# Thresholded attention and a gated feed-forward block on one core: the order of all tasks sought anew, with other durations for four kinds of task

## The chip, the core and the metric

The kernel runs on one core of a Trainium2 chip. A core has a matrix engine (PE, called TensorE), a vector engine (DVE), a scalar engine (ACT), a general engine (POOL, called GpSimd) and a sequencer for transfers (SP, called SyncE). Each takes its own instructions in the order in which they were written into its list, and waits on semaphores for the others. On-chip memory is SBUF (128 partitions); PE writes its results into PSUM. The metric is the device time of one execution in microseconds (us), the median over runs; less is better.

## What is computed

The reference first does attention on 8 batches of 8 heads, 576 positions and 64 values a head, keeping only scores within tau of the row's maximum, and then a feed-forward block on the 4608 rows that result.

```python
scores = scale * np.matmul(q, k.transpose(0, 1, 3, 2))
thresh = np.max(scores, axis=-1, keepdims=True) - tau
scores = np.where(scores >= thresh, scores, -1000000000.0)
scores = scores - np.max(scores, axis=-1, keepdims=True)
attn = np.exp(scores)
attn = attn / (np.sum(attn, axis=-1, keepdims=True) + 1e-09)
x = np.matmul(attn, v)            # (8, 8, 576, 64), then turned into (4608, 512)
h = x @ w_in                      # (512, 2048)
g = h * (1.0 / (1.0 + np.exp(-1.702 * h)))
return g @ w_out                  # (2048, 512)
```

All of it is in float32.

## The kernel before

**The work on a pair of heads.** Heads are taken in 32 pairs, n = 0 to 31, four to a batch. SP loads q, k and v (`load_qk`, L446 to L457, and `load_v`, L468). For the first four pairs PE turns q and k with a unit matrix (`turn_in`, L565 and L568) and ACT and DVE copy the result out of PSUM (`turned`, L580 and L578); for the later ones DVE turns them (`prep`, L556). PE forms the scores, transposed, in nine pieces (`scores`, L590). ACT copies each piece into SBUF (`keep`, L607), so that a pair has four full tiles of 1152 columns and one half tile of 576. DVE takes the maximum of each tile (`in_groups`, L613) and over the tiles (`over_tiles`, L622). The maximum over the partitions is an exchange between groups of 32: ACT copies four (or two) small pieces across (`cross_max`, L632) and DVE joins them (`over_halves`, L639). The result is spread over a tile on DVE (`spread_max`, L651), or, for pair 1 and pairs 3 to 6, sent through DRAM by transfers of POOL (L646, L647, L663, L672), which for some tiles are also added to the scores by an accumulating transfer (`add_row`, L678). DVE subtracts it (`sub`, L687), ACT does the mask (`mask`, L694) and the exponential (`exps`, L698). PE multiplies with v (`values`, L709). The row sums are products with a matrix of ones for the first four pairs (`sums_by_pe`, also L709, results in `den`); for later pairs DVE adds (`in_groups`, L613, `over_tiles`, L622), ACT exchanges (`cross_sums`, L764), DVE inverts (L769 to L773) and transfers send the row out and back spread (`sums_out`, L778, and `sums_in`, L785). DVE scales the values with it and places them as the input of the feed-forward block (`place_x`, L813).

**One block of PE for two pairs.** From pair 6 on, the values of an earlier pair and the scores of pair n are one block of PE: eight L709 and eight L590 in turn, nothing else between them. From pair 7 on the earlier pair is n - 1. Up to pair 16 such a block begins when all exponentials of the earlier pair are over.

**The weights.** w_in and w_out come in 16 pieces each (`load_w`, L510), and each piece is converted by two steps on ACT (`cv_power`, L520, and `cv_power2`, L524) and two on DVE (`cv_whole`, L538, and `cv_end`, L545).

**The feed-forward block.** It goes over the 4608 rows in blocks of 256. The first two blocks are plain products: L876 and L887 for the first matrix, with ACT (`tanh`, L843) and DVE (`gelu_0`, L893) behind them, L856 for the second, copied out by ACT (`half`, L863). All later ones take seven products of quarters in place of eight (L955, L1097, L1248 for the first matrix; L1397, L1357 for the second), with sums of quarters on DVE and ACT (L969, L974, L1013 to L1024, L1419). For this, sums of quarters of the weights are built once: ACT copies a quarter (`w_copy`, L922, for w_in; `t_minus`, L997, for w_out), and an accumulating transfer of POOL adds the other (`w_plus`, L926, and `t_plus`, L1001, 1 MB each). There are four of each, and each waits for the one before.

**Products of ones.** PE also does 88 small products of a matrix of ones with itself (`stay_warm`, L1463, 44 tasks of two), whose results are not used. They have the lowest rank of all.

**What sets the order.** The kernel builds a list of tasks, each with its engine, a duration in us, a rank, the tasks that it waits for and the buffers that it takes and gives back. `run_in_order` then plays this list through with the durations that the tasks carry: whenever an engine is free, the ready task of least rank runs next, and its instructions are written into the engines' lists at that moment. The order is thus fixed when the kernel is built; the chip doesn't change it. A task's rank is the number of its pair plus a bias by the name of its function: `EARLY` for pairs 0 to 3, `SECOND` for 4 to 7, `LATER` from 8 on, `CV` for weight pieces. `W_RANK` and `L_RANK` rank the loads of weights and of q, k and v. Products of the feed-forward block have the rank `LAST` (1000): PE does them when no attention task is ready.

```python
if rank != FIRST and rank < LAST and f not in (first_act, tau_terms, run_up, stay_warm):
    biases = EARLY if a[0] < NPAIR else SECOND if a[0] < 2 * NPAIR else LATER
    rank += CV[f.__name__] if f.__name__ in CV else biases.get(f.__name__, 0.0)
```

Of the kernel before, what the change touches and what calls it, by code (L numbers as in the profile page):

```python
# [32 lines left out]
def kernel(  # L33
# [96 lines left out]
    for x in ("raw0", "raw1", "qkT0", "qkT1", "mb"):  # L130
# [6 lines left out]
        "add_row": -16.97,  # L137
        "cross_max": -20.65,
        "exps": 41.44,
        "in_groups": -70.53,  # L140
        "keep": -47.19,
        "load_qk": 48.52,
        "load_v": 47.71,
        "mask": 87.96,
        "one_row": 0.3,
        "over_halves": 0.45,
        "over_tiles": -10.52,
        "place_x": 37.44,
        "row_in": 46.59,
        "row_out": 59.74,  # L150
        "scores_run": -87.56,
        "spread_max": 71.07,
        "spread_sums": 153.92,
        "sub": 40.08,
        "sums_by_pe": 1.52,
        "turn_in": 15.11,
        "turn_rows": 0.21,
        "turned": 66.22,
        "values": 60.02,
    }  # L160
    SECOND = {
        "add_row": -30.98,
        "cross_max": -5.57,
        "cross_sums": 40.19,
        "exps": 292.23,
        "in_groups": 939.1,
        "keep": -76.76,
        "load_qk": 18.7,
        "load_v": 63.05,
        "mask": 42.23,  # L170
        "over_halves": -41.03,
        "over_tiles": -26.57,
        "place_x": -8.57,
        "prep": 26.61,
        "row_in": 40.59,
        "row_out": 35.52,
        "scores_run": -43.88,
        "spread_max": -18.91,
        "sub": 135.33,
        "sums_in": 34.0,  # L180
        "sums_out": 41.84,
        "turn_rows": 96.96,
        "turn_sums": 176.66,
        "values": 15.56,
    }
    LATER = {
        "add2": -35.99,
        "add3": -111.96,
        "copy2": -83.6,
        "copy3": -8.15,  # L190
        "cross_max": 47.26,
        "cross_sums": 50.04,
        "exps": 44.03,
        "in_groups": 94.92,
        "keep": -19.43,
        "load_qk": 20.35,
        "load_v": -38.75,
        "mask": -10.73,
        "over_halves": 16.72,
        "over_tiles": 100.01,  # L200
        "place_x": 73.6,
        "prep": 141.22,
        "s_level1": -14.23,
        "s_level2": -24.56,
        "scores_run": 9.16,
        "silu2": -52.07,
        "spread_max": -56.97,
        "sub": 11.52,
# [2307 lines left out]
```

## Time and profile before

| | us |
|---|---|
| runs of the kernel before: median (lowest, highest of 3) | 1228.22 (1226.78, 1228.65) |
| the profiled execution, its own time | 1225.56 |
| span of the profile of that execution | 1223.8 |
| ACT busy, whole span | 800.8 |
| DVE busy, whole span | 1059.3 |
| mean traffic to and from the DMA engines | 112 GB/s |

A row in order of time gives the start in us from the beginning of the span, the duration, the engine, the line, the operation, what it writes and reads, the shape, and how many instructions were merged into it; in brackets stands how long the engine had been idle before it, and what ended that. "PEld" is the load of the fixed operand of a matmul, "q" behind an engine's name its sequencer. PE's instructions overlap each other, so one of them is longer than the pace at which they follow. One product in the kernel is two matmuls in the trace, as the operands are float32. A buffer is named without its number: `arena` stands for two large regions that hold most tiles.

### The profile page before, as it was taken

To read this page: it belongs to the slowest core of one execution; us is meant where nothing else is said; L and a number is where in the kernel's file an instruction comes from. 1 tells how busy PE (TensorE), PEld (TensorE's weight loads), DVE (VectorE), ACT (ScalarE), POOL (GpSimd) and SP (SyncE) were. 2 spreads that over 40 slices of the span, in tenths; PEclk is the share of its full clock that TensorE was granted. 3 is DMA by queue.
4 is the path that set the end of the run, shared out by engine and by line. 5 is a ranking of instruction groups with operands and counts; after the bars stand their busy time and mean duration, and the time that the engine had idled before them with its cause. 6 is when DMAs were issued, how large, how long until landed. Compare 5 with 4: busy or idle time off the path is not lost.

```text
span 1223.8 us, 26074 instructions
## 1 busy us (share of the span) xinstructions
PE 1211.3 (99%) x10592; PEld 980.2 (80%) x10592; DVE 1059.3 (87%) x1649; ACT 800.8 (65%) x1201; POOL 71.9 (6%) x115
## 2 busy tenths in 40 slices
PE   8999999999999999999999999999999999999999
PEld 6557764587888888887777877787887797999999
DVE  6898987778889998999879786788789889999797
ACT  6999998576676767665677376747875676440340
POOL 0111222110000000000000010001100000000000
PEclk9999999999999999999999999999999999999999
DMA  8848659873313233233432242224422341344443
GB/s 218 218 99 220 171 154 181 191 153 75 109 30 109 48 88 81 74 97 102 122 84 69 71 125 74 75 54 118 101 50 67 98 128 53 125 130 135 146 135 104
DMA packets 202232, 137.12 MB, mean 112 GB/s; under 512 B 146880, under 2 KB 164416, under 8 KB 201984
## 3 DMA queue, kind: packets, MB, share of 16 engines
q1 hardware_dynamic: 189712, 110.21, 33.7%
q0 software_dynamic: 11712, 24.95, 9.9%
q8 instruction: 83, 1.36, 0.5%
q10 hardware_dynamic: 688, 0.30, 0.1%
q14 instruction: 37, 0.30, 0.1%
HBM read 103.28 MB, written 23.75 MB: 104 GB/s over the span
## 4 chain that ended last, share of the span: by engine, by line
PE 80%; issue 1%; ACT 0%; DMA 0%; DVE 0%; POOL 0%; POOLq 0%; DVEq 0%; ACTq 0%
PE ops L1397 24%; PE pv L709 9%; PE ps L590 8%; PE hps L955 7%; PE hps L1097 7%; PE ps L955 5%; PE ps L1097 5%; PE ops L1357 4%; PE hps L1248 4%; PE ps L1248 3%; PE ps L1357 3%; DMA arena<-row_s 0%; ACT arena L694 0%; DVE arena L687 0%; ACT arena L698 0%
## 5 line engine op out<-in xcount | busy, mean ns | idle before, releaser
L613 DVE TRANSPOSE_TENSOR_REDUCE part<-arena 128x36 f32<-128x1152 f32 (+1 forms) x300 | 365.0, 1241 | 75.0 <-ACT arena L607 58.5
L607 ACT COPY arena<-ps 128x576 f32<-128x576 f32 x288 | 170.9, 642 | 112.0 <-PE ps L590 111.6
L694 ACT ACTIVATE arena<-arena 128x1152 f32<-128x1152 f32 (+1 forms) x160 | 165.9, 1062 | 55.8 <-DVE arena L687 55.5
L687 DVE TENSOR_TENSOR arena<-arena 128x1152 f32<-128x1152 f32 (+1 forms) x150 | 180.4, 1243 | 0.7
L698 ACT ACTIVATE arena<-arena,shift 128x1152 f32<-128x1152 f32 (+1 forms) x160 | 178.9, 1154 | 1.2
L590 PE MATMUL ps<-arena 64*64 64x288 f32 x2304 | 172.1, 410 | 5.4 <-ACT arena L607 2.6
L1397 PE MATMUL ops<-w_out,arena 128*128 128x256 f32 x768 | 173.1, 380 | 0.0
L1397 PEld LDWEIGHTS ops<-w_out,arena 128*128 128x128 f32 x768 | 144.7, 190 | 23.0 <-issue 3.9
L709 PE MATMUL pv<-arena 64*64 64x288 f32 x2176 | 158.1, 405 | 0.0
L590 PEld LDWEIGHTS ps<-arena 64*64 64x64 f32 x2304 | 83.3, 133 | 65.4 <-ACT arena L607 19.9
L709 PEld LDWEIGHTS pv<-arena 64*64 64x64 f32 x2176 | 80.4, 133 | 52.8 <-issue 7.5
L1397 PE MATMUL ops<-arena 128*128 128x256 f32 x528 | 118.5, 380 | 0.0
L1397 PEld LDWEIGHTS ops<-arena 128*128 128x128 f32 x528 | 100.1, 190 | 14.8 <-issue 1.3
L632 ACT ACTIVATE other<-red,minus_gap 32x18 f32<-32x18 f32 x118 | 36.2, 307 | 52.4 <-DVE red L622 51.1
L1262 ACT COPY arena<-hps 128x512 f32<-128x512 f32 x44 | 25.8, 585 | 59.3 <-PE hps L1248 58.8
L856 PE MATMUL ops<-w_out,arena 128*128 128x512 f32 x128 | 55.9, 594 | 0.0
L1074 POOL DMA_DIRECT2D arena<-wrow x36 | 19.4, 540 | 592.4 <-PE ops L1397 395.7
L887 PE MATMUL hps<-xT,w_in 128*128 128x256 f32 x232 | 50.8, 380 | 0.0
L887 PEld LDWEIGHTS hps<-xT,w_in 128*128 128x128 f32 x232 | 43.9, 190 | 6.8 <-issue 0.9
L856 PEld LDWEIGHTS ops<-w_out,arena 128*128 128x128 f32 x128 | 24.1, 190 | 30.1 <-issue 28.9
L955 PEld LDWEIGHTS hps<-xT,w_in 128*128 128x128 f32 x384 | 44.4, 192 | 1.1 <-issue 0.5
L955 PE MATMUL hps<-xT,w_in 128*128 128x128 f32 x384 | 45.1, 275 | 0.1
(228 smaller groups left out, 1909.2 us busy)
## 6 DMA issues: line engine op xcount, KB each, us to landing
arena<-in_v_dram SPq DMA_DIRECT2D x128, 144.0 KB
arena<-exu SPq DMA_DIRECT2D x42, 256.0 KB
arena<-ext SPq DMA_DIRECT2D x39, 256.0 KB
arena<-wrow POOLq DMA_DIRECT2D x36, 256.0 KB, 3.0
arena<-in_k_dram SPq DMA_DIRECT2D x112, 72.0 KB
arena<-in_q_dram SPq DMA_DIRECT2D x112, 72.0 KB
out_dram<-osb SPq DMA_DIRECT2D x28, 256.0 KB
arena<-row_s SPq DMA_DIRECT2D x48, 144.0 KB
```

The source lines that it names most:

```text
L590: nc.tensor.matmul(ps[ts(c, KT), h, 0:SH], lhsT=mats[n, 1][ts(h, D), ts(j, KT)], rhs=mats[n, 0][ts(h, D), ts(c, SH)], start=True, stop=True,)
L607: nc.scalar.copy(out=sT[n, t][:, u], in_=pss.pop((n, j))[:, :, 0:SH])
L613: nc.vector.tensor_reduce(out=stats[n, op][:, t * 2 * QB : min(2 * t + 2, NK) * QB], in_=sT[n, t].rearrange("p u h (g d) -> p (u h g) d", ...
L687: engine.tensor_tensor(out=s, in0=s, in1=mbs[n].unsqueeze(1).to_broadcast(list(s.shape)), op=ALU.add if n in BY_DMA else ALU.subtract,)
L694: nc.scalar.activation(out=s, in_=s, func=AF.Prelu, alpha=STEEP)
L698: nc.scalar.activation(out=s, in_=s, func=AF.Exp, scale=SCALE, bias=shift)
L709: nc.tensor.matmul(o[c][ts(h, D), 0:SH], lhsT=left(j, h)[ts(c, KT)], rhs=sT[n, t][ts(c, KT), u, h, :], start=(j == 0), stop=(j == NK - 1),)
L887: nc.tensor.matmul(hidden[j][:, ts(i, BLK)], lhsT=w_in[:, c, ts(j, P)], rhs=xTs[i][:, c, :], start=(c == 0), stop=(c == NDC - 1), skip_gro ...
L955: nc.tensor.matmul(o[:, ts(j, HT)], lhsT=left[:, c, ts(4 * y + j, P)], rhs=right[:, c, :], start=(x in (P1, P2, P5) and j + c == 0), stop= ...
L1097: nc.tensor.matmul(o[:, ts(j, BLK)], lhsT=left[:, c, ts(j, P)], rhs=right[:, c, :], start=(x in (P1, P2, P5) and j + c == 0), stop=(j + c ...
L1248: nc.tensor.matmul(o[:, ts(j, HT)], lhsT=left[:, ts(j, P)], rhs=right, start=(m in (P1, P2, P5) and j == 0), stop=(j == 3), skip_group_che ...
L1397: nc.tensor.matmul(banks[blk][k][:, ts(o, HM)], lhsT=left[:, j, :], rhs=right[:, j, :], start=(j == 0), stop=(j == HF - 1),)
```

## The change

The code of every task is the same. Changed are numbers in the tables of biases, the ranks of the loads, the durations of some tasks in the list, and one dependence: the small products of ones no longer wait each for the one before, only for the first one.

- All values of `EARLY`, `SECOND`, `LATER` and `CV`, of `W_RANK` and of `L_RANK` are new.
- `cross_max` (the exchange of maxima): 0.45 to 0.55 where two pieces are exchanged, 0.85 to 1.2 where four are.
- `cv_power` 0.68 to 0.75 and `cv_power2` 0.65 to 0.56.
- `turn_in` of pairs 1 to 3: 0.75 and 1.3 to 0.6 and 1.2.
- `stay_warm`: 0.25 to 0.26.

```diff
     LATER = {
-        "add2": -35.99,
-        "add3": -111.96,
...
+        "add2": -48.46,
+        "add3": -25.71,
...
-    W_RANK = (127.9, 169.1, 75.25, 398.03, -20.4, -11.42)
+    W_RANK = (76.72, 196.12, 138.01, 508.95, -9.25, -19.99)
...
-        m = task("ACT", 0.68, rank, cv_power, i, after=[a] + over)
-        m = task("ACT", 0.65, rank, cv_power2, i, after=[m])
+        m = task("ACT", 0.75, rank, cv_power, i, after=[a] + over)
+        m = task("ACT", 0.56, rank, cv_power2, i, after=[m])
...
-                task("PE", ((0.75, 1.35) if n == 0 else (0.75, 1.3))[x], r, turn_in, n, x, after=y, take=("psA",), give=own(n, f"raw{x}"))
+                task("PE", ((0.75, 1.35) if n == 0 else (0.6, 1.2))[x], r, turn_in, n, x, after=y, take=("psA",), give=own(n, f"raw{x}"))
...
-                    "PE", 0.25, LAST + 1.0, stay_warm, x, after=warmth[-1:] + [pq, pk],
+                    "PE", 0.26, LAST + 1.0, stay_warm, x, after=warmth[:1] + [pq, pk],
...
-            "ACT", 0.45 if quick else 0.85, r, cross_max, n, after=[a, tau_done] + crossed["max"],
+            "ACT", 0.55 if quick else 1.2, r, cross_max, n, after=[a, tau_done] + crossed["max"],
```

What this does to the engines' lists, as they are built (the same instructions in another order; a product counts once here):

```
PE before, from the first L887 on          PE after, from the first L887 on
68 L887, 6 L876                            76 L887, 6 L876
  block of values and scores                 block of values and scores
48 L887, 12 L856                           40 L887, 2 L856
  values of pair 5                           values of pair 5
8 L856                                     24 L856
  block                                      block
28 L856                                    32 L856
  block                                      block
16 L856, 48 L955                           6 L856, 112 L955, 4 L1397
  block                                      block
64 L955, 24 L1397                          48 L1397
  block                                      block
32 L1397, 48 L955                          8 L1397, 112 L955
  block                                      block
64 L955, 28 L1397                          48 L1397
...
```

On DVE, the placing of pair 6's values (L813) stands behind pair 7's subtractions before, and ahead of pair 7's L651 after.

More of the change, by code (lines that the diff above doesn't have):

```diff
@@ L155 @@
[L155 to L159, printed above, removed]
+        "add_row": 53.65,
+        "cross_max": 41.92,
+        "exps": 6.51,
+        "in_groups": -32.22,
+        "keep": -15.97,
+        "load_qk": -22.11,
+        "load_v": 171.75,
+        "mask": 55.94,
+        "one_row": -16.46,
+        "over_halves": 4.98,
+        "over_tiles": 6.84,
+        "place_x": 20.81,
+        "row_in": 57.26,
+        "row_out": 46.57,
@@ L160 @@
+        "scores_run": -10.81,
+        "spread_max": 80.7,
+        "spread_sums": 100.15,
+        "sub": 57.71,
+        "sums_by_pe": -23.63,
+        "turn_in": 17.28,
+        "turn_rows": 22.22,
+        "turned": 23.53,
+        "values": 13.65,
     }
     SECOND = {
[L162 to L170, printed above, removed]
@@ L185 @@
+        "values": -8.21,
     }
     LATER = {
[L187 to L203 removed]
```

99 lines of the change are left out of this document (52 added, 47 removed).

## The prediction

> **What bounds the kernel now.** I read four views in this order: the page's busy times and chain of waits, a table of busy time by stage, the engines' lists of instructions in order of time, and groups of instructions by line. For the changed kernel I have only its order of instructions on each engine, compared with the order before.
>
> ```profile
> PE 1211.3 (99%) x10592; PEld 980.2 (80%) x10592; DVE 1059.3 (87%) x1649; ACT 800.8 (65%) x1201; POOL 71.9 (6%) x115
> ...
> PE 80%; issue 1%; ACT 0%; DMA 0%; DVE 0%; POOL 0%; POOLq 0%; DVEq 0%; ACTq 0%
> ```
>
> ```profile
> 0.00:50.00 50.00, 44.47 (x704) 31.32 (x708) 37.45 (x53) 38.15 (x57) 8.10 (x23) 0.97 0.89 238
> 50.00:100.00 50.00, 45.95 (x664) 25.38 (x656) 43.45 (x78) 49.52 (x70) 9.31 (x14) 1.00 0.50 106
> 100.00:150.00 50.00, 50.00 (x351) 39.88 (x348) 48.80 (x72) 48.51 (x75) 11.05 (x15) 1.00 0.85 217
> ...
> 1150.00:1200.00 50.00, 50.00 (x450) 50.00 (x450) 47.82 (x93) 17.98 (x38) 0.00 (x0) 1.00 0.47 133
> ```
>
> The columns after the window are busy us (and instructions) of PE, PEld, DVE, ACT, POOL, then clock, DMA share and GB/s. PE is never idle from 100 us on; all its idle time (50 - 44.47 and 50 - 45.95, 9.6 us) lies ahead. There ACT is full: 49.52 of 50. So the time is the moment at which PE becomes dense plus a fixed amount of matmul work, as long as no new wait opens later. The dense stretch begins here, with its first ACT answer 1.9 us later:
>
> ```profile
> 94.45 0.77 ACT L698 ACTIVATE arena<-arena,shift 128x576 f32<-128x576 f32 x1
> ...
> 104.62 0.61 ACT L843 ACTIVATE xT<-hps 128x512 f32<-128x512 f32 x1
> ```
>
> ```profile
> 102.73 1.13 PE L887 MATMUL hps<-xT,w_in 128*128 128x256 f32 x4
> ```
>
> **The change part by part.** No instruction is added or removed: both orders hold the same matmuls by line (1152 of L590, 1296 of L709, 88 of L1463 and so on), the same vector and scalar work. The changed durations and ranks only move work. I count what is moved.
>
> 1. *The stretch ahead of L887.* Up to the first L843, ACT has the same instructions in both orders, but for the weight conversions: 10 L520 and 9 L524 before, 12 and 11 after. Their pace when they run back to back, and the time ACT was idle in between:
>
> ```profile
> 145.65 1.45 ACT L520 ACTIVATE w_out<-arena,rebias 128x512 f32<-128x512 int16 x2
> ...
> 148.71 3.19 ACT L524 ACTIVATE w_out<-w_out,rebias 128x512 int32<-128x512 f32 x5
> ```
>
> ```profile
> 9.47:95.22 85.75, 80.77 (x115) 0.98 0.72 179
> 95.22:104.62 9.40, 9.37 (x17) 1.00 0.78 150
> ```
>
> ```profile
> 16.03 0.76 ACT L520 ACTIVATE w_in<-w_out,rebias 128x512 f32<-128x512 int16 x1 [0.69 <-DMA w_out<-in_moe_w_in_dram]
> ...
> 26.52 0.64 ACT L632 ACTIVATE other<-red,minus_gap 32x18 f32<-32x18 f32 x2 [1.82 <-DVE red L622]
> ...
> 29.65 1.17 ACT L694 ACTIVATE arena<-arena 128x1152 f32<-128x1152 f32 x1 [1.00 <-DVE arena L687]
> ...
> 38.20 0.64 ACT L607 COPY arena<-ps 128x576 f32<-128x576 f32 x1 [0.27 <-PE ps L590]
> ```
>
> One L520 more costs about 0.67 us (1.45 for two, the last with its tail), one L524 about 0.62 ((3.19 - 0.72) / 4): two of each put 2.6 us more ACT work ahead of L843. Against it stand the 4.98 us (85.75 - 80.77) in which ACT was idle between its first score copy at 9.47 and the last exponential of pair 3 at 95.22; four waits are 3.8 of them, the rest are hand-overs of some 0.05 us. The new order seems to remove the four: the query block of pair 2 is loaded and turned earlier, all of pair 1's copies run ahead of the four L632 of pair 0, so that these find their L622 done, and three L520 stand where ACT waited for pair 1's. The first weight is asked for behind fewer loads, so the 0.69 goes too. DVE's list up to its first L687 is shorter by one L578 and one L545:
>
> ```profile
> 17.57 0.41 DVE L538 TENSOR_SCALAR w_out<-w_out 128x512 int32<-128x512 uint32 x1
> 18.09 0.69 DVE L545 SCALAR_TENSOR_TENSOR w_in<-w_out,w_in 128x512 int32<-128x512 int32 x1
> ...
> 28.27 5.83 DVE L687 TENSOR_TENSOR arena<-arena 128x1152 f32<-128x1152 f32 x5
> ```
>
> I take 2.6 - 3.8 = -1.2 us for the start of the dense stretch. Bounds: every idle moment gone, 2.6 - 4.98 = -2.4; every one kept or replaced, +2.6. I take the inner value because hand-overs stay and nothing in the new order shows a wait that must take their place.
>
> 2. *The products of ones.* Before, 82 of the 88 products run ahead of 102.73, four stand in the tail and two after the last product. After, all run early, in waits of PE. The four in the tail:
>
> ```profile
> 1053.88 1.06 PE L1248 MATMUL hps<-xT,w_in 128*128 128x128 f32 x8
> 1054.87 0.94 PE L1463 MATMUL up<-ones 64*64 64x64 f32 x8
> 1055.74 1.16 PE L1248 MATMUL hps<-xT,w_in 128*128 128x128 f32 x8
> 1056.73 1.06 PE L1248 MATMUL ps<-xT 128*128 128x128 f32 x8
> ```
>
> Groups of eight L1248 follow each other at 0.89 us elsewhere here; from 1053.88 to 1055.74 is 1.86 and the next step 0.99, so the four cost 1.07 us. They were put there because PE was expected to wait at that place, and the trace can't show whether it would have: between 0 and -1.07, I take -0.5. The last two end beside the final vector add and set nothing.
>
> 3. *Order within the dense stretch.* Between the blocks in which PE does scores and values of a pair of heads, L955 and L1397 are distributed anew: before each gap holds 28 L1397 and 48 or 64 L955, after it is mostly 48 L1397 in one gap and 112 L955 with 8 L1397 in the next. The entries into and out of such blocks are equal in number (two fewer in the tail, counted above), so the PE work is the same: 0, as long as the softmax of a pair fits into the shorter gap. That gap is 96 matmuls of the trace (two for each product):
>
> ```profile
> 666.89 36.46 PE ops L1397 x168
> ```
>
> 36.46 / 168 x 96 = 20.8 us. What has to fit, by pair 10, whose block ends where L1397 takes over:
>
> ```profile
> 296.88 3.29 PE L1397 MATMUL ops<-w_out,arena 128*128 128x256 f32 x14
> ```
>
> ```profile
> 299.30 1.26 ACT L632 ACTIVATE other<-red,minus_gap 32x18 f32<-32x18 f32 x4 [1.59 <-DVE red L622]
> 306.69 1.16 ACT L694 ACTIVATE arena<-arena 128x1152 f32<-128x1152 f32 x1 [6.12 <-DVE arena L687]
> 307.89 1.26 ACT L698 ACTIVATE arena<-arena,shift 128x1152 f32<-128x1152 f32 x1
> ...
> 315.64 3.06 ACT L698 ACTIVATE arena<-arena,shift 128x1152 f32<-128x1152 f32 x3
> ```
>
> ```profile
> 302.88 0.95 DVE L813 TENSOR_TENSOR xT<-pv,arena 128x128 f32<-128x128 f32 x4 [1.71 <-DMA arena<-row_s]
> 304.43 0.77 DVE L651 STREAM_TRANSPOSE arena<-red 128x576 f32<-128x576 f32 x1
> ```
>
> ```profile
> 1.89 1.28 ACT L1451 ACT_TABLE_LOAD   x1 [1.89 <-issue]
> ```
>
> After, L651 stands right behind L639 in these gaps (L813 comes earlier): L632 is over at 300.56, 3.7 us after the block; L639, L651 and the first L687 take some 2.2 and their hand-overs 0.5, so masks begin 6.4 us after the block, not 9.8. A mask and an exponential follow each other in some 2.3 us (1.16 and 1.26 with their tails): 9.2 for four tiles, 1.25 for the half tile, 1.28 for a table load, which now falls into this gap: 11.7. The exponentials end 18.1 us after the block, 2.7 us before 20.8. No stall; L632's own duration in the planner was raised, which only places the next block later. The end (last product, two adds, a store) is the same instructions in both.
>
> Sum: -1.2 - 0.5 + 0 = -1.7 us. The profiled execution took 1225.56 us, of which 1223.8 are the span; 1225.56 - 1.7 = 1223.9. The median of the runs is 2.66 us above the profiled one (1228.22), so I forecast 1226.5.
>
> **Rivals.**
> *A. All idle time goes and nothing stood in the tail:* -2.4 - 1.07 = -3.5, which is 1224.7. For it: ACT, at 49.52 of 50 in the second stage, is the only bound there. Against: hand-overs are in any order.
>
> *B. The change doesn't do what it says:* ACT waits elsewhere as long as before, +2.6 - 0.5 = +2.1, 1230.3. For it: pair 3's keys are now loaded behind seven weight pieces, in a stage where DMA is 0.89 busy. Against: on PE their turn stands behind 34 products of ones, which leaves them time.
>
> *C. The sums of rows lie behind the weight sums.* POOL's list before:
>
> ```profile
> 203.20 0.89 POOL L926 DMA_DIRECT2D arena<-arena  x1 [3.00 <-DMA row_s<-flat_s]
> 208.12 1.27 POOL L785 DMA_DIRECT2D arena<-row_s  x2 [4.03 <-DVE arena L687]
> ```
>
> ```profile
> DMA to landing us min/median/max: 9.1/10.6/13.6
> ```
>
> The second view is of the four L926. Before, pair 6's L785 waits until pair 7's subtractions are over, and nobody hurries. After, DVE's list has L813 of pair 6 ahead of L651 of pair 7, so that pair's softmax waits for a row that lands behind the second L926; the third and fourth L922 on ACT stand among pair 7's exponentials and each waits for the L926 before. The two blocks in question, and the pace of the work between them:
>
> ```profile
> 186.90 1.20 PE L709 MATMUL pv<-arena 64*64 64x288 f32 x16
> ...
> 195.87 19.58 PE L856 MATMUL ops<-w_out,arena 128*128 128x512 f32 x45
> ...
> 220.10 1.20 PE L709 MATMUL pv<-arena 64*64 64x288 f32 x16
> ```
>
> A product of L856 is 0.87 us (two of 45 in 19.58). Six more stand ahead of the first block and ten ahead of the second, so with the start at -1.2 they begin at 190.9 and 227.6. The second pair of L922 is done after four score copies of the first block, near 197.5; a landing of 9.5 (near the short end: the others came close behind another transfer) gives 207.0 and 209 for the third pair, 218.7 for the third L926, 221 for the fourth pair; the last mask and three exponentials of pair 7 behind it end at some 225.7, 1.9 ahead of the block. With 13.6 for both transfers they come 8.2 later and PE waits 6: -1.7 + 6 = +4.3, 1232.5. It decides from a landing of about 10.5.
>
> The Trainium skill (DMA: Bandwidth & Descriptors, section Anatomy of one DMA — SWDGE (gpsimd) path) fits such a transfer with 2.0 us plus the bytes at 436e3 per us, an estimate of 4.4 us for this 1 MB. By it C could not occur and the sum would stay -1.7. The trace disagrees, 9.1 us at the least; these transfers accumulate, which may be why.
>
> *D. The shorter gap is too short.* If the softmax takes what it took for pair 10 (318.70 - 296.88 = 21.8 us, with the wait for a row and vector work in between) and the table load on top, it is 23.1 against 20.8: 2.3 us in each of three gaps, 6.9 - 1.7 = +5.2, 1233.4. It decides from 20.8 us. Against it: those gaps carry little other vector work (six L1419), and L813 is out of the way.
>
> **How the numbers follow.** Chances: forecast 0.42, A 0.20, B 0.13, C 0.12, D 0.13. About 0.2% (2.5 us) is what a measurement tells from no change: faster is below 1225.8, slower above 1230.7. The forecast's own range, 1225 to 1228.5, gives a third of its chance to faster and the rest to no change; A three quarters to faster; B half to slower, half to no change; C and D four fifths to slower. That makes faster 0.30, no change 0.44, slower 0.26. The range leaves out the lower end of A and the upper ends of C and D: 1223 to 1233.
>
> **What would show it.** Step 1: L887 starts at 101.5 (100.3 to 105.3), ACT's idle time between its first L607 and pair 3's last L698 near 1.2 us. Step 2: no L1463 after L887, and no idle PE in its place near 1054. Step 3: no idle time of PE ahead of L709 after 100 us; in the gaps of 48 L1397 the last L698 ends 2 to 3 us ahead of L709. C would show as PE idle ahead of one L709 near 228, behind ACT L698; D as the same at three blocks. I am wrong if PE stands still in the dense stretch, or if the start moves by more than 2.6.

## The result, and the profile after

| | before | changed |
|---|---|---|
| median of 22 executions each, us | 1226.99 (1225.4 to 1228.93) | 1224.95 (1223.74 to 1229.24) |
| ratio of the times, 95% interval | | 0.9984 (0.9977 to 0.999) |
| profiled execution, own time / span | 1225.56 / 1223.8 | 1225.39 / 1223.6 |

The change makes the kernel 2.0 us faster (1.2 to 2.8 by the interval). The two profiled executions differ by only 0.2 us: that of before was among the fastest of its kernel, that of the changed kernel was slower than its median. Most of this section and two of the experiments are about that gap, since a single profile of each would have told a wrong story. Below, the head is what lies ahead of the first L887, where the dense stretch of PE begins, and the tail is what lies behind the last attention block.

The changed kernel's page, busy times and shares of the chain of waits:

```profile
PE 1212.8 (99%) x10592; PEld 987.0 (81%) x10592; DVE 1059.3 (87%) x1649; ACT 803.1 (66%) x1203; POOL 71.0 (6%) x115
...
PE 92%; ACT 4%; DMA 2%; DVE 1%; issue 0%; SPq 0%; POOL 0%; POOLq 0%
```

Its busy time by stage (columns as in the prediction: PE, PEld, DVE, ACT, POOL, clock, DMA share, GB/s):

```profile
0.00:50.00 50.00, 46.56 (x712) 37.36 (x716) 38.73 (x56) 41.30 (x62) 7.82 (x23) 0.97 0.90 234
50.00:100.00 50.00, 46.41 (x670) 28.85 (x666) 44.79 (x78) 49.52 (x70) 10.25 (x16) 1.00 0.62 134
100.00:150.00 50.00, 49.86 (x353) 39.57 (x350) 49.49 (x72) 49.78 (x76) 9.87 (x14) 1.00 0.75 202
...
1050.00:1100.00 50.00, 49.59 (x445) 49.43 (x444) 48.55 (x96) 23.34 (x43) 0.00 (x0) 1.00 0.44 132
```

PE is busy 46.56 us in the first stretch (44.47 before) and 46.41 in the second (45.95 before): 2.5 us less idle time ahead of 100 us, of which the six products of ones that moved here fill a part. The last row is new: 0.41 us of idle PE in the tail.

Both kernels were profiled again. The four profiles, cut at the same pieces of work:

| us | before | before, again | changed | changed, again | mended (below) |
|---|---|---|---|---|---|
| first score copy L607 on ACT | 9.47 | 9.35 | 9.35 | 8.99 | 8.66 |
| first L887, the start of the dense stretch | 102.73 | 102.17 | 102.29 | 102.90 | 100.67 |
| from there to the last attention block | 942.12 | 942.52 | 942.76 | 942.65 | 941.86 |
| from there to the end of the last product L1357 | 175.84 | 175.84 | 175.38 | 175.42 | 175.28 |
| mean granted clock of that execution | 0.999 | 1.000 | 0.999 | 0.997 | 1.000 |

The mended kernel has the order of the changed one up to 600 us, so its start is a third sample of the changed head. Four kernels of the experiments, edited only further back, have this head too: they start the dense stretch at 101.00, 101.32, 101.39 and 101.87. So one and the same order starts it anywhere between 100.67 and 102.90; the mean of the seven is 101.63, that of the two profiles of before 102.45. What is seen to vary is a transfer and the clock. In the changed kernel's second profile PE waits for the keys of pair 3, and the clock falls right there:

```profile
35.30 0.78 PE L1463 MATMUL up<-ones 64*64 64x64 f32 x10
37.48 2.18 PE L568 MATMUL ps<-eye,arena 64*64 64x64 f32 x32 [1.40 <-DMA arena<-in_k_dram]
```

```profile
35.00:37.50 2.50, 1.10 (x19) 0.99 (x17) 2.50 (x4) 2.47 (x3) 2.50 (x5) 0.87 0.99 290
37.50:40.00 2.50, 2.50 (x42) 2.44 (x46) 0.64 (x2) 2.47 (x3) 1.60 (x2) 0.50 1.04 355
40.00:42.50 2.50, 2.50 (x27) 2.50 (x23) 2.49 (x5) 2.47 (x4) 0.00 (x0) 0.50 1.04 285
42.50:45.00 2.50, 2.50 (x37) 2.50 (x34) 2.50 (x7) 2.09 (x4) 0.00 (x0) 0.76 1.09 298
```

The clock column reads 0.87, 0.50, 0.50, 0.76: at one half for 6.8 us, from the wait of 1.40 on. In the mended kernel's profile the same products follow without a wait, and the clock stays at 1.00:

```profile
35.33 0.42 PE L1463 MATMUL up<-ones 64*64 64x64 f32 x4
35.59 1.44 PE L568 MATMUL ps<-eye,arena 64*64 64x64 f32 x32
```

So it is worth comparing executions of the same mean granted clock. With a mean of 1.00 the median of before is 1225.74 (16 of 79 executions in all sessions) and of the changed kernel 1223.87 (13 of 33): 1.9 us apart, close to the 2.0 of the medians above. With a mean of 0.999 it is 1226.82 (29) and 1225.22 (10): 1.6 us apart. With a mean under 0.9985 it is 1226.77 (34) and 1226.07 (10): 0.7 us apart. The new order gains more where the clock holds.

### The profile page after: what moved, and what is told of

It reads as the page before. It is cut to its first block, busy times and chain, and to the rows that moved or that the text cites. A ratio compares the mean times of both kernels' runs of the same rounds, so it can differ in the third digit from the quotient of the medians.

```text
span 1223.6 us, 26039 instructions
## 1 busy us (share of the span) xinstructions
PE 1212.8 (99%) x10592; PEld 987.0 (81%) x10592; DVE 1059.3 (87%) x1649; ACT 803.1 (66%) x1203; POOL 71.0 (6%) x115
## 4 chain that ended last, share of the span: by engine, by line
PE 92%; ACT 4%; DMA 2%; DVE 1%; issue 0%; SPq 0%; POOL 0%; POOLq 0%
PE ops L1397 24%; PE pv L709 10%; PE ps L590 10%; PE hps L955 7%; PE hps L1097 7%; PE ps L955 5%; PE ps L1097 5%; PE ops L856 5%; PE hps L887 4%; PE ops L1357 4%; PE hps L1248 4%; PE ps L1357 3%; PE ps L1248 3%; ACT arena L694 1%; ACT arena L698 1%; ACT arena L607 1%
## 5 line engine op out<-in xcount | busy, mean ns | idle before, releaser
L613 DVE TRANSPOSE_TENSOR_REDUCE part<-arena 128x36 f32<-128x1152 f32 (+1 forms) x300 | 363.8, 1239 | 65.9 <-ACT arena L607 49.0
L607 ACT COPY arena<-ps 128x576 f32<-128x576 f32 x288 | 170.5, 644 | 96.8 <-PE ps L590 96.8
L590 PE MATMUL ps<-arena 64*64 64x288 f32 x2304 | 171.4, 408 | 3.4 <-ACT arena L607 3.1
L709 PE MATMUL pv<-arena 64*64 64x288 f32 x2176 | 158.5, 405 | 0.0
L590 PEld LDWEIGHTS ps<-arena 64*64 64x64 f32 x2304 | 82.2, 132 | 64.1 <-ACT arena L607 25.3
L709 PEld LDWEIGHTS pv<-arena 64*64 64x64 f32 x2176 | 82.2, 133 | 52.2 <-issue 9.1
L632 ACT ACTIVATE other<-red,minus_gap 32x18 f32<-32x18 f32 x118 | 36.2, 307 | 39.0 <-DVE red L622 37.6
L887 PE MATMUL hps<-xT,w_in 128*128 128x256 f32 x232 | 50.8, 380 | 0.0
L887 PEld LDWEIGHTS hps<-xT,w_in 128*128 128x128 f32 x232 | 43.9, 190 | 6.8 <-issue 0.4
L955 PEld LDWEIGHTS hps<-xT,w_in 128*128 128x128 f32 x384 | 44.2, 192 | 1.1 <-issue 0.9
L955 PE MATMUL hps<-xT,w_in 128*128 128x128 f32 x384 | 44.9, 275 | 0.0
```

Source lines behind the costliest of these rows:

```text
L590: nc.tensor.matmul(ps[ts(c, KT), h, 0:SH], lhsT=mats[n, 1][ts(h, D), ts(j, KT)], rhs=mats[n, 0][ts(h, D), ts(c, SH)], start=True, stop=True,)
L607: nc.scalar.copy(out=sT[n, t][:, u], in_=pss.pop((n, j))[:, :, 0:SH])
L613: nc.vector.tensor_reduce(out=stats[n, op][:, t * 2 * QB : min(2 * t + 2, NK) * QB], in_=sT[n, t].rearrange("p u h (g d) -> p (u h g) d", ...
L709: nc.tensor.matmul(o[c][ts(h, D), 0:SH], lhsT=left(j, h)[ts(c, KT)], rhs=sT[n, t][ts(c, KT), u, h, :], start=(j == 0), stop=(j == NK - 1),)
L887: nc.tensor.matmul(hidden[j][:, ts(i, BLK)], lhsT=w_in[:, c, ts(j, P)], rhs=xTs[i][:, c, :], start=(c == 0), stop=(c == NDC - 1), skip_gro ...
L955: nc.tensor.matmul(o[:, ts(j, HT)], lhsT=left[:, c, ts(4 * y + j, P)], rhs=right[:, c, :], start=(x in (P1, P2, P5) and j + c == 0), stop= ...
```

## The experiments

All kernels but the first three and `costs_only` take the changed kernel's order of tasks, edit it in a few places and play it; every task and all other places stay. The hook, with `behind(a, b)` putting task a right behind task b:

```diff
-                tasks[i][3](*tasks[i][4])
+                order.append(i)
...
+        [tasks[i][3](*tasks[i][4]) for i in edited(order, tasks)]
```

**The same kernels again.** No edit.

> The kernel before, unchanged, to see how far its own executions differ. Its profiled execution was at 1225.56 us, 1.4 below its median of 1226.99, that of the changed kernel at 1225.39, 0.4 above its median of 1224.95. If the order alone sets the stretch ahead of the first product L887, that starts within 0.3 us of 102.73 again and the dense stretch takes 1121.1 us to the end of the span. Rival: transfers or the granted clock move the start by 1 us or more from one execution to the next, and the difference of the medians (2.0 us) lies there, not in what the two profiles show (0.2 us).

> The changed kernel, unchanged, for the same question: first L887 at 102.29 within 0.3 us, three blocks of values and scores (near 614.8, 748.4 and 882.0) 0.3 us longer than the others, one wait of PE near 1055, if these belong to the order; by the rival, the start differs by 1 us or more. Time 1224.95 within 0.7 us.

Measured: 1226.78 (ratio to before 0.9999, 0.999 to 1.0007) and 1224.62 (0.9985, 0.9977 to 0.9994). What belongs to the order came back: in the changed kernel the blocks at 615.26, 748.87 and 882.48 take 9.28 us again from their first matmul to that of the next product, where an undisturbed block takes 8.97, and PE waits near 1055. The start did not: 102.17 and 102.90. The rival holds for the two profiles; the medians stand.

**The products of ones alone.**

```diff
-                    "PE", 0.25, LAST + 1.0, stay_warm, x, after=warmth[-1:] + [pq, pk],
+                    "PE", 0.26, LAST + 1.0, stay_warm, x, after=warmth[:1] + [pq, pk],
```

> Before, with one dependence changed: the products of ones wait only for the first one (and 0.26 for 0.25), all other numbers as before. Step 2 of the prediction: no L1463 after L887; the last feed-forward stretch takes 175.4 to 175.7 us in place of 176.21 (0.5 us less, with a wait of PE of 0.4 to 0.6 us where the four products stood), or 175.1 (all of 1.07) if nothing stood there to wait for, or 176.2 if the wait takes all of it. The head keeps its waits, so that L887 starts at 102.7 within 0.6; time 0.5 us below before, 1226.5. If all of the gain of the change came from the products of ones, the time would be 1225.

Measured: 1228.05 where 1226.5 was expected, ratio 1.0013 (1.0004 to 1.0022), slower. The tail takes 175.41, as expected, with the wait of 0.41 by the profile's count where the products stood. But the dependence alone moves more than that: all 88 products are now chosen ahead of the first L887, which stands at 103.47, the first block of values and scores stands at 130.27 and takes 9.75 us (9.22 before), and from the first L887 to the last attention block it takes 943.95 us, 0.65 of them for eight score matmuls more than before. So the tail's part of the gain comes with this edit, but the gain of the change doesn't come from it alone, and one edit of a list that is played through can't be expected to stay local.

**The four products back in the tail.**

```diff
+    for i in (pick("stay_warm", 43), pick("stay_warm", 42)):
+        behind(i, pick("product2", 14, 1, 3))
```

> The changed kernel with two of the 44 tasks of products of ones (four products) put back in the tail, where PE stood still 0.58 us near 1055. The stretch from the end of the last attention block to PE's last product took 175.38 and 175.42 us in two executions of the changed kernel, and 175.84 of before up to its last product L1357. If step 2 is right as a sum (the four products cost 1.07 us and cover a wait of 0.58), it takes 175.9 us, 0.5 more, and no wait of PE is left there. Rival: the products only fill the wait and cost nothing (175.4), or the wait comes behind them again (176.5).

Measured: 175.92 us for the stretch. The tail of the changed kernel, then of this one:

```profile
1054.08 1.06 PE L1248 MATMUL hps<-xT,w_in 128*128 128x128 f32 x8
1055.55 1.13 PE L1248 MATMUL hps<-arena 128*128 128x128 f32 x8 [0.41 <-DVE arena L1220]
```

```profile
1053.57 1.06 PE L1248 MATMUL hps<-xT,w_in 128*128 128x128 f32 x8
1054.56 0.94 PE L1463 MATMUL up<-ones 64*64 64x64 f32 x8
1055.56 1.16 PE L1248 MATMUL hps<-arena 128*128 128x128 f32 x8
```

From one group of eight to the next it is 1.47 us in the changed kernel (0.89 elsewhere, so 0.58 of waiting) and 1.99 here (1.10 for the products). The products cover the wait and cost 0.5 us on top: the sum of step 2 holds.

**A wait put back in the head.**

```diff
+    last = pick("cross_max", 1)
+    for i in (pick("cv_power", 1), pick("cv_power2", 0), pick("cv_power", 2)):
+        behind(i, last)
+        last = i
```

> The changed kernel with three weight conversions (two L520, one L524) put behind the two L632 of pair 1 instead of ahead of them, so that ACT has nothing to do while DVE works towards the L622 of pair 1: the wait of 1.82 us of before is back in the changed order. Step 1 of the prediction: ACT stands still 2.0 us there (the three took 22.81 to 24.87), all that follows on ACT is that much later, and so is the first L887: 2.0 us less what later waits take up (0.76 us were left in front of a later L694), so 1.2 to 2.0 us over the changed kernel, 1226.0 to 1226.8, and 102.0 to 102.7 for L887 at full clock (100.67 in the undisturbed execution of the mended kernel). Rival: idle moments of ACT in the head aren't what sets the start, the conversions find room later: 0 to 0.3 us.

```profile
23.58 0.64 ACT L632 ACTIVATE other<-red,minus_gap 32x18 f32<-32x18 f32 x2 [1.32 <-DVE red L622]
24.25 0.79 ACT L520 ACTIVATE w_in<-w_out,rebias 128x512 f32<-128x512 int16 x1
```

Measured: 1225.6, ratio to before 0.9994 (0.9985 to 1.0004), so the gain of 2.0 shrinks to some 0.8, and the interval reaches from a gain of 1.8 to a loss of 0.5. At full clock it is 1225.43 (3 executions) against 1223.87 of the changed kernel, 1.6 more, inside the 1.2 to 2.0 expected; the median over all, 1225.6, lies below the 1226.0 to 1226.8 expected. The first L887 stands at 102.64, the upper end of what was expected, but the head without this edit has been seen at 102.90 too. ACT's wait is 1.32, not 2.0: L622 was ready sooner. The rest came through PE, which then waits 1.94 us for a score copy (to 28.11) and has a clock of 0.69 and 0.63 in the two stretches from 27.5 to 32.5 us. That ACT's idle time in the head sets the start is borne out by the times at full clock, and by the sum over all profiles further below; here the wait also made PE wait, and the clock fell behind it.

**The changed durations alone.** Before, with all changed durations and the changed dependence, and every rank as before.

> Before, with the changed durations and the changed dependence of the products of ones alone, all ranks and biases as before. If the traced durations as such make the order better, the time is that of the changed kernel, 1224.9, within 1 us. Rival: the ranks were found for a set of durations, and the same ranks with other durations give an order that nobody looked for: 1227 to 1230, with waits of PE within the dense stretch (a gap of 45 L1397 and one of 40 L1397 are shorter than any of the changed kernel) and a first L887 at or behind 102.7.

Measured: 1260.57, ratio 1.0277 (1.0261 to 1.0292). The rival, and far beyond its numbers: the first L887 is at 110.51, and behind 100 us PE stands still 21.9 us in 16 waits, and its clock is at one half for 20.5 us. These durations are worth something only with ranks that were sought for them; the new ranks with the old durations were not run.

**Rival C forced.**

```diff
+    behind(pick("sums_in", 6), pick("w_plus", 2))
+    behind(pick("place_x", 6), pick("sums_in", 6))
```

> Rival C of the prediction, forced: in the changed kernel POOL issues the transfers that spread the row of pair 6's sums (L785) behind the third weight sum (L926) instead of behind the second, and L813 of pair 6 goes with them, still ahead of L651 of pair 7. The row landed at 208.87; behind the third L926 (217.70) it lands near 219, 10 us later, and the last exponential of pair 7 goes from 225.7 to near 235.7. As the prediction has it (the block needs all exponentials, 1.9 to 2.5 us of slack): PE waits 7.5 us ahead of or in the block of 228.2. Rival: the block needs one tile after the other and the scores between need only their buffers; its last values are wanted 8 us after its start, so PE waits 2 to 5 us. If nothing waits for that row: 0.

PE and ACT of this kernel:

```profile
229.22 1.15 PE L709 MATMUL pv<-arena 64*64 64x288 f32 x16
237.58 2.20 PE L590 MATMUL ps<-arena 64*64 64x288 f32 x16 [7.21 <-ACT arena L607]
...
231.37 3.05 ACT L698 ACTIVATE arena<-arena,shift 128x1152 f32<-128x1152 f32 x3
236.44 0.42 ACT L764 COPY other<-red 32x18 f32<-32x18 f32 x2 [2.02 <-DVE red L622]
```

Measured: 1233.75 in one execution. The block at 227.23 takes 18.36 us in place of 9.04, 9.3 more; pair 7's last exponential ends at 234.4. That is close to what the prediction's theory says (7.5), but only in part for its reason. PE doesn't wait for a tile of values: those need one tile after the other, as the rival says. It is held by a score buffer, from 230.37 to 237.58. ACT copies scores out (L607) only behind the exponentials, which end 4.1 us into this wait, and behind L764, the exchange of the row sums of pair 7. L764 stands ahead of the copies on ACT and waits 2.02 us for DVE's sums of all five tiles, so it is over another 2.4 us later. And 2.1 of the 9.3 us aren't waiting at all, but matmuls at half the clock:

```profile
235.00:237.50 2.50, 0.00 (x0) 0.00 (x0) 1.91 (x6) 1.02 (x4) 0.00 (x0) 0.50 1.08 223
237.50:240.00 2.50, 2.42 (x20) 1.29 (x24) 1.50 (x2) 1.36 (x4) 1.08 (x2) 0.50 1.11 217
```

**Rival D in three doses.** The last one, two and three tasks of products (with the adds that use them) go behind the block.

```diff
+    for n, blk, count in ((9, 2, 1), (11, 3, 2), (15, 5, 3)):
+        last = pick("scores_run", n + 1, [8])
+        for c in ((5, (0, 4)), (5, (4, 8)), (6, (0, 4)))[3 - count :]:
+            last, x = pick("product", blk, *c), last
+            behind(last, x)
...
```

> Rival D of the prediction, in three doses within one kernel: of the 48 products L1397 in the gaps ahead of the blocks at 299.3, 366.8 and 501.8, the last 4, 8 and 12 (1.74, 3.47 and 5.21 us) are done behind the block, with the adds that use them. The last exponentials end 2.1, 2.1 and 2.0 us ahead of these blocks. If a block needs all exponentials of its pair, as the prediction has it, PE waits 0, 1.4 and 3.2 us (4.6 in all). Rival: only the first tile has to be ready and the score buffers have to come free in time (ACT copies scores out behind the last exponential): 0, 0 and 0.5 to 1.0 us, as in the blocks whose last exponential ends 2.6 us after the block's start and that are 0.32 us longer.

```profile
299.97 1.26 PE L590 MATMUL ps<-arena 64*64 64x288 f32 x16 [0.71 <-ACT arena L607]
...
367.81 1.26 PE L590 MATMUL ps<-arena 64*64 64x288 f32 x16 [1.76 <-ACT arena L607]
...
504.89 2.20 PE L590 MATMUL ps<-arena 64*64 64x288 f32 x16 [3.49 <-ACT arena L607]
```

Measured: 1233.41; the three blocks take 10.03, 11.09 and 15.45 us, so 1.0, 2.05 and 6.4 more than 9.04. Both theories miss it: PE stands still already at the first dose, where the last exponential ends 0.3 us ahead of the block. The third block again pays for a fallen clock (its groups of L590 take 2.20 in place of 1.15). The list of ACT names the holder, the same as before:

```profile
497.18 4.20 ACT L698 ACTIVATE arena<-arena,shift 128x1152 f32<-128x1152 f32 x4
503.75 0.42 ACT L764 COPY other<-red 32x18 f32<-32x18 f32 x2 [2.38 <-DVE red L622]
504.20 1.18 ACT L607 COPY arena<-ps 128x576 f32<-128x576 f32 x2
```

**The holder moved.** The shortened gaps, with L764 behind the first two score copies at these three places.

```diff
+    for n in (9, 11, 15):
+        last = pick("keep", n + 1, 1)
+        for name in ("cross_sums", "turn_sums", "sums_out"):
+            behind(pick(name, n), last)
+            last = pick(name, n)
```

> The kernel with the three shortened gaps, where PE waited 1.0, 2.05 and 6.4 us in the blocks, with one more edit at these three places: ACT does the exchange of the row sums (L764) behind the first two score copies (L607) of the next pair instead of ahead of them. Theory: L764 waits for L622, which stands behind five sums L613 on DVE, and every score copy waits behind L764, so that PE finds no free score buffer; the last exponential isn't what decides. With the edit the copies follow the last exponential: 0, 0 and about 1.1 us (it ends 0.3 us ahead of the first block and 1.4 and 3.1 us behind the start of the others). Rival: PE waits for the exponentials or for buffers that the sums hold: 1.0, 2.05 and more as before.

```profile
298.25 1.18 ACT L607 COPY arena<-ps 128x576 f32<-128x576 f32 x2 [2.08 <-PE ps L590]
299.46 0.42 ACT L764 COPY other<-red 32x18 f32<-32x18 f32 x2
...
501.20 0.42 ACT L764 COPY other<-red 32x18 f32<-32x18 f32 x2 [1.33 <-DVE red L622]
```

Measured: 1226.28 (one execution), 7.1 below the kernel without the edit. The blocks take 9.04, 9.15 and 10.88 us: 0, 0.1 and 1.8 more. The theory holds: with L764 out of the way the first two gaps could be up to 3.5 us shorter at no cost. The third has 0.7 us more than expected; its two waits are 0.55 and 0.72, the second behind L764 once more, as only two copies were put ahead of it.

**Three blocks and the tail mended.**

```diff
+    behind(pick("add2", 14, ("g", 1, 0, 1), ("p5", 0)), pick("x_sum1", 14, 1))
+    for nth, n in enumerate((18, 22, 26)):
+        for x in (2, 3):
+            behind(pick("keep4", x, 2, nth=nth), pick("keep", n + 1, x - 2))
```

> The changed kernel with six copies of ACT (two L1138 each at the pairs 18, 22 and 26) put behind the last exponential and the first score copies, and one vector add of the tail (L1265) behind the sum L1220 that PE waits for. Theory: the blocks near 614.8, 748.4 and 882.0 lose 0.32 us each because PE waits for a score buffer that ACT copies out late, behind those copies; they come down to 9.04 us (-0.95 in all), and the wait near 1055 (0.58) goes: 1.5 us less, 1223.4. Rival: the copies are needed where they stood, their products wait after the block instead, and the vector add frees a buffer that PE needs next: 0 to 0.3 us less.

The block of pair 18 in the changed kernel, on PE, and ACT beside it:

```profile
616.76 1.15 PE L709 MATMUL pv<-arena 64*64 64x288 f32 x16
617.94 1.25 PE L590 MATMUL ps<-arena 64*64 64x288 f32 x16
...
616.12 0.57 ACT L1138 COPY arena<-hps 128x512 f32<-128x512 f32 x1
616.58 0.78 ACT L698 ACTIVATE arena<-arena,shift 128x576 f32<-128x576 f32 x1
617.26 1.17 ACT L607 COPY arena<-ps 128x576 f32<-128x576 f32 x2
```

L590 follows L709 after 1.18 us in place of 0.97: the first score copies come at 617.26, behind two L1138 and the last exponential, 2.5 us after the block's start at 614.77. In the mended kernel the three blocks take 9.05 us in place of 9.28 (from the first matmul to that of the next product; 8.97 undisturbed): 0.23 of 0.31 us each is gone, 0.7 together. The tail gains 0.1 only. The wait goes to a later group, which starts 0.1 us after the end of DVE's L1231 (1056.42), and DVE has no idle moment there. The profile names no releaser for this wait, so that L1231 ends it is read from the times alone:

```profile
1055.18 1.06 PE L1248 MATMUL ps<-arena 128*128 128x128 f32 x8
1056.52 1.13 PE L1248 MATMUL hps<-arena 128*128 128x128 f32 x8 [0.28 <-issue]
```

```profile
1055.81 0.61 DVE L1231 TENSOR_TENSOR arena<-arena 128x128 f32<-128x128 f32 x2
```

Measured: 1224.14, ratio 0.998 (0.9972 to 0.9989); at full clock 1223.13 (4 executions), 0.7 below the changed kernel, as much as the three blocks give together. This is the fastest kernel of the study, though the intervals of the two overlap.

**The keys sooner, alone and with the mended places.**

```diff
+    last = pick("load_w", 3)
+    for i in (pick("load_qk", 3, 1), pick("load_qk", 3, 1, nth=1)):
+        behind(i, last)
+        last = i
```

> The changed kernel with SP's loads of pair 3's keys (L446) issued ahead of the weight pieces 4, 5 and 6 instead of behind them, some 4 us earlier. Theory: the executions of the changed kernel differ by how long PE waits for these keys near 36 to 37.5 us. In five of them: waits of 0, 0.2, 0.7, 1.1 and 1.4 us with the first L887 at 100.7, 101.0, 101.3, 102.3 and 102.9, and where the wait is over 0.6 the granted clock is at a half for 3.4 or 6.8 us behind it. Without the wait the start is 100.7 to 101.0 in nearly every execution, most executions show a mean clock of 1.00, and the median comes down from 1224.8 to that of the executions of the changed kernel at full clock, 1223.9. Rival: the weight pieces and the values of pair 1 that come later make ACT, DVE or PE wait instead, or the clock falls for another reason: 1224.8 or more.

> The edit of the keys and the edits of the mended kernel together. The mended kernel was at 1224.14, at full clock at 1223.13. If the keys were what held its other executions, the median is 1223.1 within 0.4, 3.7 below before. Rival: 1224.1.

Measured: 1225.26 (ratio 0.9992, 0.9983 to 1.0001) and 1224.17 (0.9982, 0.9973 to 0.9991). Half of the theory holds: 19 of 22 executions have a mean clock of 1.00 now (13 of 33 in the changed kernel), and no profile shows a wait for these keys. But the time doesn't come down; at full clock it is 1225.24 and 1224.10. In the first kernel's profile, which is the fastest of its 11 executions (1224.01), nothing took the place of the wait, and the first L887 stands at 101.03. In the second's it stands at 103.38, and the profile shows what took the place, on DVE and on ACT:

```profile
45.12 0.43 DVE L538 TENSOR_SCALAR w_out<-w_out 128x512 int32<-128x512 uint32 x1 [2.48 <-DMA w_out<-in_moe_w_in_dram]
45.46 1.35 DVE L687 TENSOR_TENSOR arena<-arena 128x1152 f32<-128x1152 f32 x1
...
46.84 1.16 ACT L694 ACTIVATE arena<-arena 128x1152 f32<-128x1152 f32 x1 [2.08 <-DVE arena L687]
```

A weight piece that was moved back by the keys lands later, L538 waits for it on DVE, and pair 1's subtraction stands behind L538. PE then waits 2.04 us for an exponential. From 35 to 45 us the DMA share is about 1.0 in every row above, so a load that is earlier there makes another later, as here. That this holds the other executions too is not shown.

## Why the prediction was right, and where its steps failed

1. *The start, -1.2 predicted.* Right in kind; in the two profiles without a fallen clock it is 102.17 before and 100.67 after, -1.5. But 100.67 is the earliest of the seven profiles of this head; by the means, 102.45 and 101.63, it is -0.8. ACT's idle time between its first L607 and the last exponential of pair 3 was to fall from 4.98 to about 1.2 us; in the two executions without a fallen clock it is 4.73 and 1.19:

```profile
9.35:94.66 85.31, 77.42 (x1176) 46.99 (x1168) 75.71 (x112) 80.58 (x115) 12.15 (x16) 1.00 0.71 180
```

```profile
8.66:94.03 85.37, 79.50 (x1200) 48.97 (x1192) 78.01 (x116) 84.18 (x121) 13.45 (x18) 1.00 0.79 195
```

The first is before (again), the second the mended kernel with the changed head; ACT's busy time is the fourth (80.58 of 85.31, 84.18 of 85.37). With the 9.37 and 8.06 us from there to the first L843, ACT is busy 89.95 and 92.24: the added work was 2.3 us, not 2.6. The mechanism, that the start moves with ACT's idle time, is borne out by all profiles. In the ten that have the changed head, as it is or with a wait put back or the keys sooner, the first L887 less the first L607 less ACT's idle time between is 90.8 to 91.3 us, while the idle time goes from 1.19 to 3.26; in the two of before it is 88.3 and 88.1. The 2.8 us between are the added work and a first L843 that comes 0.5 us sooner behind the first L887. What the prediction took too low is the idle time of most executions: it is 1.19 in two of the seven profiles, 1.46 to 2.74 in the five in which PE waited 0.67 us or more for the keys of pair 3, and 1.69 on average. A term that was missing is one that the prediction took as fixed: the first L607 itself. The new order loads the keys of pair 0 ahead of its queries, and ten executions of that head start L607 between 8.64 and 9.35, the two of before at 9.35 and 9.47. What the step also lacked is the spread, 100.67 to 102.90, more than the whole forecast.

2. *The products of ones, -0.5 predicted.* Measured -0.46 and -0.42 for the stretch, and 0.5 when they were put back. That the number fits is luck: the prediction knew only the two bounds and took the middle. The step's own sign to look for, "no idle PE in its place", was wrong: half of the price being paid by a wait means that the wait shows, and it does (0.58).

3. *The order in the dense stretch, 0 predicted.* Measured from the first L887 to the last attention block: 942.12 and 942.52 before, 942.76 and 942.65 after, +0.4. Three blocks that begin before their last exponentials are over, at gaps of 56 L1097, lose 0.31 each, 0.9. Of the remaining -0.5 a part is short waits of PE that only the profiles of before have, 0.35 us for L893 near 113.7 in the second and 0.13 ahead of an L955 near 244.8 in the first; the rest was not followed up. Nor is the work quite the same, as the prediction has it: ACT has 1203 instructions after and 1201 before, the two more being table loads; no wait of PE was traced to them. The failed term is the slack: "the exponentials end 18.1 us after the block, 2.7 us before 20.8". They end 18.8 after it (278.44 to 297.2), 2.1 ahead. The time is lost ahead of the masks, which begin 7.2 us after the block in place of 6.4: L813, which was to be out of the way, now stands on DVE ahead of the last L613 and the L622 that L632 waits for, and L632 is over 4.5 us after the block, not 3.7.

```profile
279.55 0.91 DVE L813 TENSOR_TENSOR xT<-pv,arena 128x128 f32<-128x128 f32 x4
...
281.18 0.43 DVE L622 TENSOR_REDUCE red<-part 128x18 f32<-128x162 f32 x1
```

```profile
281.64 1.27 ACT L632 ACTIVATE other<-red,minus_gap 32x18 f32<-32x18 f32 x4 [0.85 <-DVE red L622]
285.66 1.16 ACT L694 ACTIVATE arena<-arena 128x1152 f32<-128x1152 f32 x1 [2.75 <-DVE arena L687]
```

Nor is the last exponential what decides. In the first dose of the shortened gap a shift of 1.74 us cost 1.0: the margin was 0.7 us, held by L764 and DVE's sums, which the prediction left out since nothing in the profile of before waited there.

*Rivals.* A (all idle time gone, nothing to wait for in the tail) didn't come, though its time, 1224.7, is nearer to the measured 1224.95 than the forecast is: at least 1.19 us of idle time stay in the head, and PE waits 0.58 in the tail. B named the right place, the keys of pair 3: the 34 products of ones ahead of them were to leave them time, and in the profiles they came 0 to 1.4 us too late. C's chain was timed well (last exponential of pair 7 at 225.7, as predicted; block at 228.17 in place of 227.6; the transfers in question landed 8.4 and 8.8 us after their issue, under the 10.5 from which it decides), and the forced run shows the price: exponentials that end 9.7 us later against their block (7.2 behind its start in place of 2.5 ahead of it) made PE wait 7.2 us. That this is the number of the prediction's own arithmetic is in part chance, since PE waits for the copies behind them and for L764; 2.1 us of half clock come on top. D didn't occur at the gaps it named, but was nearer than priced: 0.7 us, not 2.7.

Together: -1.7 predicted; by the medians -2.0 (-1.2 to -2.8). The profiles give -1.5 - 0.4 + 0.4 = -1.5 with the earliest start and -0.8 with the mean of the starts, so they account for the medians only in part; two profiles of before, both faster than its median, are too few for more. The forecast of 1226.5 lies 1.55 us above the measured 1224.95, mostly for another reason: it started from the median of three executions, 1228.22, and the median of 22 is 1226.99. The prediction also took 2.5 us as the least that a measurement tells from no change and so gave no change the greatest chance, 0.44, and faster only 0.30; with 22 executions each, 2.0 us is told from nothing.

## What to carry to other kernels

Slack is not the distance to the last producer by name: look at what stands in the waiting engine's list ahead of the instruction that frees the buffer (here an exchange of row sums ahead of the score copies), since an in-order list makes every later instruction wait for it. A new plan is ranks and durations together; taking over the durations without the ranks was 34 us slower than before, and one dependence alone was slower too. Where the differences are a fifth of a per cent, profile both kernels more than once and compare executions of the same granted clock before explaining a difference of two profiles.

## What the runs showed of the hardware

The granted clock falls to one half in portions. During or shortly behind PE's waits for the keys of 0.67, 0.8, 1.06 and 1.3 us in four profiles of the changed head, and behind the 1.94 of the wait put back, it was at 0.50 for 3.4 us; from the wait of 1.40 on, and from the waits of 3.49 and 7.21 us in the dense stretch on, for 6.8 us (worked out from the clock column: the lost share of each row over 0.5). Waits of 0.71 and 1.76 us inside a block of values and scores had no such effect, and the wait of 2.0 us that both profiles of before show in the head (L590 for L580) was followed by 3.4 us of it in the one and by none in the other. Nor does the length of one wait decide within the head: a wait of 0.74 to 0.76 us for a score copy near 26 us, which all profiles of the changed head but that of the wait put back have, was never followed by a fall in the next 9 us, nor was the wait of 2.04 us in the kernel with the keys sooner and the mended places, here between 64x288 products:

```profile
49.35 1.20 PE L709 MATMUL den<-arena,ones 64*64 64x288 f32 x16 [2.04 <-ACT arena L698]
```

```profile
47.50:50.00 2.50, 0.65 (x12) 0.48 (x16) 2.47 (x4) 2.47 (x3) 0.00 (x0) 1.00 1.07 247
```

The rows around the wait of 3.49 us in the kernel with the shortened gaps:

```profile
500.00:504.80 4.80, 1.40 (x24) 0.61 (x16) 4.21 (x8) 2.39 (x6) 0.00 (x0) 0.87 0.00 0
504.80:507.00 2.20, 2.11 (x20) 1.18 (x24) 1.51 (x2) 1.22 (x3) 0.00 (x0) 0.50 0.04 10
507.00:509.00 2.00, 2.00 (x24) 1.07 (x20) 1.17 (x1) 0.64 (x1) 0.00 (x0) 0.50 0.34 89
509.00:511.00 2.00, 2.00 (x26) 1.04 (x24) 0.21 (x1) 0.85 (x2) 0.00 (x0) 0.66 0.21 58
```

The Trainium skill (TensorE: Matmul & The Clock Gate, section Part 1: The HAM clock gate (the "warmup" mystery)) knows two clock states, full and half, set by free-running windows of about 3.4 us of activity; the 0.50, the portions of 3.4 and 6.8 us and the two profiles of before agree. Its rule under HAM oscillation — how this bites in real kernels, that idle gaps of PE above some 3.4 us are the ones to avoid, is too lenient here: in all five profiles of the changed head with a wait for the keys of 0.67 us or more the clock fell within 1.5 us of that wait's end, without any wait of PE over 1.40 there, and in the four that have neither such a wait nor the wait put back it stayed at 1.00 there. What else must come together with the wait is open; whether small products count as little activity was not tried.
